# Four attention layers on one core: q and k projected in products of 512 columns, normalized rows in two tiles, maxima woven over the last two steps

## The chip, the cores and the metric

The kernel runs on one core of one Trainium2 chip. The metric is device time in microseconds (us) of one launch; of several runs the median counts. TensorE (PE in the profile) multiplies, and loads the weights of each product first (PEld); VectorE (DVE), ScalarE (ACT) and GpSimd (POOL) work on tiles; SyncE (SP) issues the transfers. Each engine runs its own instructions in the order in which the program wrote them, and waits at an instruction until what it needs is there.

## What is computed

Four layers with a residual connection, alternately of two kinds. A has 32 heads with their own keys and values, B has 32 heads of queries and one head of keys and values. All is float32, with 2048 tokens, a width of 576 and heads of 18.

```python
x = A_x
x = x + _A_ref(_layernorm(x, axis=-1), A_wqkv, A_wo)
x = x + _B_ref(_layernorm(x, axis=-1), B_wq, B_wk, B_wv, B_wo)
x = x + _A_ref(_layernorm(x, axis=-1), A_wqkv, A_wo)
x = x + _B_ref(_layernorm(x, axis=-1), B_wq, B_wk, B_wv, B_wo)
# _A_ref and _B_ref: q, k, v = projections of x
# scores = einsum("bhqd,bhkd->bhqk", q, k) * Dh ** -0.5
# o = einsum("bhqk,bhkd->bhqd", softmax(scores), v);  return o @ wo
```

## The kernel before

**Layout.** The sixteen chunks of 128 tokens lie in `xo`. A layer normalizes them (`norm`, in two stages: `stats` and `scaled`), transposes the result on TensorE (`trans`), projects it to q, k and v, runs the attention of sixteen pairs of heads over four blocks of 512 queries, and multiplies by the output weights (`out_proj`), chunk by chunk, while the chunks of the next layer are already normalized.

**Accuracy.** Each number is split in a rounded part and a rest. A projection therefore has fourteen products (`TERMS`) for each result, with transposed rows of 9 parts of 128 (`split_rows`) against weights of 10 parts. The result leaves PSUM (`project`) as a rounded part by ACT and a rest by VectorE; both go to the DRAM tile `qk_d` (`store`) and come back by head (`load_k`, `load_q`) into the slots of `big`, where the projection's weights lie too. `project(..., filler=True)` uses the PSUM buffers "e" (three) in place of "m" (two), lets ACT copy the result twice and POOL subtract, and so leaves VectorE free.

**The loop before.** It takes 256 tokens at a time (`tt` 0 to 7). Transposed rows have two tiles of 256 tokens, in turn (`xt`). `project(tt, xt, group)` computes one or two results of 128 rows by 256 tokens, next to each other in one PSUM buffer. In A there are nine results (q and k: 1152 rows) a step, and `project_v` adds the values of the step before, four products of 14 terms and 288 columns; in B there are five, and the fifth holds the last queries, the keys and the values, which `v_trans` transposes back. Between the projections stand `trans` of the next step and `norm` of the one after that: in B, `norm(tt + 2, 0)` after the second result group and `norm(tt + 2, 1)` ahead of the third.

**The last steps.** The attention of a layer starts with maxima of scores: `max_pair` multiplies for both heads of a pair (L464, `psm`), and VectorE reduces (L473, `mx`). The first 28 pairs are woven into the projections: `woven(f, left, every)` calls `f` after every so many products (`beat`). In A the fillers (values and the results 1, 2, 3, 5 of the steps 6 and 7) come last; the first eight of them (`FIRST_A`) run by themselves and the others carry the pairs. In B pairs are woven from step 4 (`MAX_B`) on, in an order of blocks (`m_first`) that follows what has been stored. Then come the exponents (L608, `pse`, with ACT's L612) and the products with the values (L633, `oacc`).

**Starts.** Layer 0 loads its weights through `load_a` (part 0, 2, 1; ACT and VectorE split them). In each A layer POOL splits the value weights into `wsm` (`load_wsm`), behind what it has to do for `norm` before, and ahead of what it has to do for `norm` after: it computes `rs`, the root, that `scaled` needs. In the layers 1 to 3 the chunks 0 and 1 are transposed within `out_proj`, at its chunk 14.

Of the kernel before, what the change touches and what calls it, by code (L numbers as in the profile page):

```python
# [18 lines left out]
P = 128  # L19
# [35 lines left out]

FIRST_A = 8
MAX_B = 4
# [15 lines left out]
def tile_kernel(ctx: ExitStack, tc: tile.TileContext, A_x, A_wqkv, A_wo, B_x, B_wq, B_wk, B_wv, B_wo, out):  # L73
# [28 lines left out]
    vbuf = cst.tile([P, NCH * H * (DH + 1)], F32, name="vbuf")  # L102
# [182 lines left out]
    xhs, xts = {}, {}  # L285

    def trans(c):
        tt, u = divmod(c, 2)
        if u == 0:
            xts[tt] = pool.tile([P, 9, 256], F32R, tag="xt", name="xt")  # L290
        xh = xhs.pop(c)
        split_rows(xts[tt][:, :, u * P:(u + 1) * P], *transposed(xh, xh[:, 512:640]))
# [31 lines left out]
    load_x(0)  # L324
    for layer in range(4):
        is_a = layer % 2 == 0
        if is_a:
            v = vbuf.rearrange("p (c h e) -> p c h e", c=NCH, h=H)
        else:
            v = vbuf[:, :NCH * (DH + 1)].rearrange("p (c h e) -> p c h e", c=NCH, h=1)  # L330


        def project(tt, xt, group, filler=False):
            t0 = tt * 256
            ps = (etile if filler else mtile)("psq").rearrange("p (m t) -> p m t", m=2)
            g = len(group)
            n = 114 if not is_a and group[0] == 4 else P
            for k, t in enumerate(group):
                w = wtile(t)
                for j, (xc, wc) in enumerate(TERMS):  # L340
                    nc.tensor.matmul(ps[:n, k, :], w[:, wc, :n], xt[:, xc, :],  # L341
                                     start=j == 0, stop=j == len(TERMS) - 1)
                    beat()
            ev = [ptile("ev", (P, 2, 256), F32R) for _ in range(2)]
            ev_f = [e.bitcast(F32) for e in ev]
            nc.scalar.activation(ev[0][:n, :g], ps[:n, :g], AF.Copy)  # L346
            if filler:
                raw = ptile("evr", (P, 2, 256))
                nc.scalar.activation(raw[:n, :g], ps[:n, :g], AF.Copy)  # L349
                nc.gpsimd.tensor_tensor(ev[1][:n, :g], raw[:n, :g], ev_f[0][:n, :g], op=OP.subtract)  # L350
            else:
                nc.vector.tensor_tensor(ev[1][:n, :g], ps[:n, :g], ev_f[0][:n, :g], op=OP.subtract)  # L352
            if not is_a and group[0] == 4:
                vt = ptile("vt", (P, 256))
                nc.scalar.activation(vt[64:82], ps[64:82, 0], AF.Copy)  # L355
                store(ev_f, 0, 64, 512, 0, t0)
                store(ev_f, 96, 96 + DH, D, 0, t0)
                vts.append((tt, vt))
            else:
                for k, t in enumerate(group):  # L360
                    if t == 4:
                        store(ev_f, 0, 64, 512, k, t0)
                        store(ev_f, 64, P, D, k, t0)
                    else:
                        store(ev_f, 0, P, t * P, k, t0)

        def store(ev_f, r0, r1, c0, k, t0):

            dst = qk_d[c0:c0 + r1 - r0, :, t0:t0 + 256]
            hi, lo = ev_f[0][r0:r1, k, None, :].to_broadcast([r1 - r0, 2, 256]), ev_f[1][r0:r1, k, :]  # L370
# [9 lines left out]
        def v_trans(tt, vt):  # L380
            pv = etile("psv")
            for u in range(2):
                nc.tensor.transpose(pv[:, u * 32:u * 32 + DH], vt[64:82, u * P:(u + 1) * P], ident[64:82, 64:82])
            nc.vector.tensor_copy(v[:, 2 * tt:2 * tt + 2, 0, :DH],
                                  pv[:, :64].rearrange("p (u e) -> p u e", u=2)[:, :, :DH])

        def project_v(tt, xt, u, h, tile_f):
            c = 2 * tt + u
            pv = natural(xt[:, :, u * P:(u + 1) * P], h, tile_f)
            nc.scalar.activation(v[:, c, 16 * h:16 * h + 16, :DH], pv.rearrange("p (e d) -> p e d", d=DH), AF.Copy)  # L390
# [47 lines left out]
        def ops(p):  # L438
# [5 lines left out]
                                   [(0, i, 2) for i in range(4)] + [(0, i, 3) for i in range(4)] +  # L444
                                   [(1, i // 2, i % 2) for i in range(4, 8)] +
# [32 lines left out]
        def max_pair():  # L478
# [4 lines left out]
            if not is_a and m_done[0] == 44:  # L483
                max_store(0, 0)
            elif not is_a and m_done[0] == 52:
                max_rows(0, 0)

        nc.gpsimd.memset(v[:, :, :, DH:], 1.0)
        if layer == 0:
            norm(0, 0)  # L490
            norm(0, 1)
            for part in (0, 2, 1):
                for c in range(5):
                    load_a(c, (part,), nc.scalar, nc.vector)
                if part == 0:
                    load_x(1)
                    trans(0)
                    trans(1)
                elif part == 2:
                    norm(1, 0)  # L500
            load_x(2)
            norm(1, 1)
        else:
            for c in outs:
# [11 lines left out]
        if is_a:  # L516
            groups = [(0, 1), (2, 3), (4, 5), (6, 7), (8,)]
            first, rest = [(6, 7), (8,), (0,), (4,)], [1, 2, 3, 5]
        else:
            groups = [(4,), (0, 1), (2, 3)]  # L520
            first, rest = [], [1, 2, 3]
        fill = []
        for tt in range(8):
            if tt == 0 and is_a:
                for c in range(5):
                    load_wsm(c, A_wqkv[:, 2 * D:])
            elif tt == 0:
                fixed_rows(k_slot(0), True)
                fixed_rows(q_slot(0), False)
            if layer == 0 and tt < 5:  # L530
                load_x(tt + 3)
            gs = groups if tt < 6 else first
            for i, g in enumerate(gs):
                if tt < 6 and i == (3 if is_a else 2):
                    norm(tt + 2, 1)
                if not is_a and tt == MAX_B and i == 2:
                    woven(max_pair, 2, 13)
                elif not is_a and tt > MAX_B and i == 1:
                    woven(max_pair, 4, 13)
                project(tt, xts[tt], g, not is_a and tt >= MAX_B)  # L540
                if is_a and tt == 7 and i == 2:
                    load_k(0, 0, 1792)
                    load_q(0, 0, 512)
                if is_a and 0 < tt < 7 and i < 2:
                    for h in range(2):
                        project_v(tt - 1, xts[tt - 1], i, h, mtile)
# [228 lines left out]
```

## Time and profile before

| what | us |
|---|---|
| runs | 5867.71, 5867.76, 5873.08; median 5867.76 |
| the profiled execution | 5869.39, its span 5867.6 |
| layer 0: to the first exponent | 229.08 |
| a layer's attention (of layer 3) | 1233.07 |
| output projection of layer 0 after its first two chunks, to the projections of layer 1 | 56.57 |
| projections of layer 1 (B) to its first exponent | 107.48 |
| projections of layer 2 (A) to its first exponent | 207.43 |

A row of the timeline gives the start within the span, the length, the engine, the line, the operation, the tiles and their shape, and how many instructions it holds; in square brackets stands how long the engine had been idle before it and what released it. The length reaches to the end of the last one's result, so the time that a run of products takes is read from the start of one row to the start of the next.

### The profile page before, as it was taken

The numbers are of one execution on the slowest core, as the hardware profiler recorded it, in microseconds if no ns is written. First come the engines' busy times: TensorE is split into PE (matmuls) and PEld (weight loads), VectorE is DVE, ScalarE is ACT, GpSimd is POOL, SyncE is SP. The second block draws the span as 40 slices with busy tenths as digits, with TensorE's granted clock in tenths as the row PEclk, the third lists the DMA queues.
The fourth block names the chain that finished last, engine by engine and source line by source line (L and its number), as shares of the span: only waits on it lengthen the run. The fifth ranks groups of instructions, "written<-read, shape, count | busy, mean of one in ns | idle before, by whom it ended". The sixth has DMA issues, their size and how long they took to land. (4 is left out here: it accounts for less than half of the span.)

```text
span 5867.6 us, 136457 instructions
## 1 busy us (share of the span) xinstructions
PE 5806.8 (99%) x55296; PEld 3003.1 (51%) x55296; DVE 5183.2 (88%) x5424; ACT 4622.0 (79%) x8952; POOL 1716.4 (29%) x2209
## 2 busy tenths in 40 slices
PE   8999999999999999999999999999999999999999
PEld 8644444444844444444696444444448444444446
DVE  4799999997599999999647999999976999999995
ACT  2588888888278888888625888888882888888885
POOL 2142232324133232233311323232332323223232
PEclk9999999999999999999999999999999999999999
DMA  6311111111320000000243111111113200000002
GB/s 191 111 43 33 35 31 35 32 31 26 120 65 23 22 20 22 21 21 24 68 137 103 45 35 31 35 32 34 30 33 120 56 23 23 22 23 19 23 14 76
DMA packets 295958, 276.66 MB, mean 47 GB/s; under 512 B 135680, under 2 KB 259896, under 8 KB 285608
## 3 DMA queue, kind: packets, MB, share of 16 engines
q1 hardware_dynamic: 295328, 267.94, 16.6%
q8 instruction: 434, 7.11, 0.5%
q14 instruction: 196, 1.61, 0.1%
HBM read 151.24 MB, written 112.56 MB: 45 GB/s over the span
## 5 line engine op out<-in xcount | busy, mean ns | idle before, releaser
L473 DVE TENSOR_REDUCE mx<-psm 128x2 f32<-128x1024 f32 x4096 | 4768.0, 1217 | 179.2 <-PE psm L464 144.9
L612 ACT ACTIVATE pt<-pse 128x512 f32<-128x512 f32 x8192 | 4314.3, 602 | 543.2 <-PE pse L608 375.4
L608 PE MATMUL pse<-big 64*128 64x512 f32 x8192 | 2447.5, 417 | 3.8 <-DMA big<-m_d 2.3
L633 PE MATMUL oacc<-pt,vbuf 128*19 128x256 f32 (+2 forms) x32736 | 2323.5, 384 | 1.9 <-ACT oc L639 1.9
L464 PE MATMUL psm<-big 62*128 62x512 f32 x8192 | 2297.1, 454 | 6.6 <-DVE mx L473 6.4
L464 PEld LDWEIGHTS psm<-big 62*128 62x128 f32 x8192 | 926.0, 184 | 1461.4 <-DVE mx L473 921.0
L608 PEld LDWEIGHTS pse<-big 64*128 64x128 f32 x8192 | 1187.1, 185 | 286.3 <-ACT pt L612 191.6
L633 PEld LDWEIGHTS oacc<-pt,vbuf 128*19 128x19 f32 x32736 | 676.1, 97 | 1023.1 <-issue 796.4
L139 POOL TENSOR_SCALAR hl<-neg 128x8 fp32r<-128x8 f32 x256 | 50.9, 199 | 2665.6 <-DVE neg L584 2665.6
L656 POOL TENSOR_TENSOR rl<-lt,mone 128x8 f32<-128x8 f32 x256 | 422.9, 1652 | 564.3 <-DMA lt<-os 564.3
L341 PE MATMUL psq<-xt,big 128*128 128x256 f32 (+1 forms) x3136 | 422.1, 290 | 18.6 <-DVE ev L352 11.7
L341 PEld LDWEIGHTS psq<-xt,big 128*128 128x128 f32 (+1 forms) x3136 | 391.4, 192 | 44.0 <-issue 20.7
L346 ACT ACTIVATE ev<-psq 128x512 fp32r<-128x512 f32 (+2 forms) x148 | 73.2, 495 | 370.9 <-PE psq L341 298.9
L139 POOL TENSOR_SCALAR os<-oc 32x512 f32<-32x512 f32 x512 | 313.2, 612 | 130.8 <-ACT oc L639 88.6
L669 POOL TENSOR_TENSOR os<-os,rb 96x512 f32<-96x512 f32 x256 | 328.9, 1285 | 20.3 <-DMA rb<-r_d 19.5
L647 POOL TENSOR_TENSOR os<-os,oc 96x512 f32<-96x512 f32 x256 | 327.3, 1279 | 21.3
L216 PE MATMUL psn<-wsm,ot 128*128 128x288 f32 x1792 | 245.8, 298 | 9.7 <-DVE xo L282 7.3
L216 PEld LDWEIGHTS psn<-wsm,ot 128*128 128x128 f32 x1792 | 241.5, 190 | 17.5 <-issue 11.5
L352 DVE TENSOR_TENSOR ev<-psq,ev 128x512 fp32r<-128x512 f32 (+2 forms) x100 | 59.7, 604 | 168.2 <-ACT ev L346 152.9
L282 DVE TENSOR_TENSOR xo<-psn,xo 128x288 f32<-128x288 f32 x128 | 58.0, 456 | 143.2 <-PE psn L216 142.2
L639 ACT ACTIVATE oc<-oacc 128x512 f32<-128x512 f32 x256 | 157.7, 616 | 28.1 <-PE oacc L633 28.1
L137 ACT ACTIVATE ot<-o 128x512 fp32r<-128x512 f32 (+1 forms) x84 | 42.5, 553 | 135.2 <-PE psn L216 68.1
(54 smaller groups left out, 1127.6 us busy)
## 6 DMA issues: line engine op xcount, KB each, us to landing
big<-qk_d SPq DMA_DIRECT2D x180, 432.0 KB
qk_d<-ev SPq DMA_DIRECT2D x192, 256.0 KB
qk_d<-ev SPq DMA_DIRECT2D x240, 128.0 KB
rb<-r_d SPq DMA_DIRECT2D x512, 36.0 KB
o_d<-os SPq DMA_DIRECT2D x512, 36.0 KB
m_d<-tr SPq DMA_DIRECT2D x1024, 2.0 KB
o<-o_d SPq DMA_DIRECT2D x64, 256.0 KB
big<-m_d SPq DMA_DIRECT2D x512, 4.0 KB
```

The source lines that it names most:

```text
L139: eng.tensor_scalar(dst, src, 1.0, 0.0, op0=OP.mult, op1=OP.add)
L216: nc.tensor.matmul(ps, lhs[:, xc, :], wsm[:, wc, h * 288:(h + 1) * 288], start=i == 0, stop=i == len(TERMS) - 1)
L341: nc.tensor.matmul(ps[:n, k, :], w[:, wc, :n], xt[:, xc, :], start=j == 0, stop=j == len(TERMS) - 1)
L464: nc.tensor.matmul(ps[:, slot], q[b:b + KM, c0:c0 + P], k[b:b + KM, kb * 512:(kb + 1) * 512], start=True, stop=True)
L473: nc.vector.reduce_max(mxs[p, u][:, r0:r1 + 1:r1 - r0], ps, axis=AX.X)
L608: nc.tensor.matmul(e, k[r:r + KE, kc * P:(kc + 1) * P], q[r:r + KE, u * 512:(u + 1) * 512], start=True, stop=True)
L612: nc.scalar.activation(pt, e, AF.Exp, scale=SCALE)
L633: nc.tensor.matmul(oacc[j:j + DH + 1, cs], v[:, kc, 2 * p + a if is_a else 0, :], pts[p, u, i][:, cs], start=kc < 2 and c0 == 0, stop=kc > ...
L639: nc.scalar.activation(oc, oacc, AF.Copy)
L647: nc.gpsimd.tensor_tensor(t[:96], t[:96], oc[:96], op=OP.add)
L656: nc.gpsimd.tensor_tensor(rl, lts.pop((p, u)), mone, op=OP.pow)
L669: nc.gpsimd.tensor_tensor(t[:96], t[:96], rb[:96], op=OP.mult)
```

## The change

A step now takes 512 tokens (`T` 0 to 3), and one product of 512 columns computes what two of 256 did. Transposed rows need two tiles of twice the size. One, `xx`, is a tile of its own and serves the output projection too; the other, `yx`, takes turns with the second half of the values of an A layer (`vy`), so that `vbuf` holds one half only. The values of the chunks 8 to 11 are therefore staged (`vst`) and copied by POOL when `yx` is free. Chunks 0 to 3 are normalized and transposed ahead of the loop. In B the keys and queries are loaded in each step, and pairs of maxima are woven over the steps 2 and 3. In A two fillers run by themselves in place of eight.

```diff
-FIRST_A = 8
-MAX_B = 4
+FIRST_A = 2
...
-    vbuf = cst.tile([P, NCH * H * (DH + 1)], F32, name="vbuf")
+    NV = NCH // 2 * H * (DH + 1)
+    vbuf = cst.tile([P, NV], F32, name="vbuf")
+    xx = cst.tile([P, 2, 9, 256], F32R, name="xx")
...
-        ots_[tt] = ot = pool.tile([P, 9, 256], F32R, tag="xt", name="ot")
+        ots_[tt] = ot = xx[:, tt % 2]
...
+    def xt_of(c):
+        T = c // 4
+        if T not in xts:
+            xts[T] = xx if T % 2 else pool.tile([P, 2, 9, 256], F32R, tag="vy", bufs=1, name="yx")
+        return xts[T][:, c // 2 % 2, :, c % 2 * P:(c % 2 + 1) * P]
...
-        def project(tt, xt, group, filler=False):
-            t0 = tt * 256
-            ps = (etile if filler else mtile)("psq").rearrange("p (m t) -> p m t", m=2)
-            g = len(group)
-            n = 114 if not is_a and group[0] == 4 else P
-            for k, t in enumerate(group):
-                w = wtile(t)
-                for j, (xc, wc) in enumerate(TERMS):
-                    nc.tensor.matmul(ps[:n, k, :], w[:, wc, :n], xt[:, xc, :],
-                                     start=j == 0, stop=j == len(TERMS) - 1)
-                    beat()
+        def project(T, t, filler=False):
+            t0 = T * 512
+            ps = (etile if filler else mtile)("psq")
+            n = 114 if not is_a and t == 4 else P
+            w = wtile(t)
+            for j, (xc, wc) in enumerate(TERMS):
+                nc.tensor.matmul(ps[:n].rearrange("p (u t) -> p u t", u=2), w[:, wc, :n], xts[T][:, :, xc, :],
+                                 start=j == 0, stop=j == len(TERMS) - 1)
+                beat()
...
-            dst = qk_d[c0:c0 + r1 - r0, :, t0:t0 + 256]
+            dst = qk_d[c0:c0 + r1 - r0, :, t0:t0 + 512]
...
         if layer == 0:
-            norm(0, 0)
-            norm(0, 1)
+            for tt in range(2):
+                norm(tt, 0)
+                norm(tt, 1)
+                if tt == 0:
+                    trans(0)
+                    trans(1)
             for part in (0, 2, 1):
                 for c in range(5):
                     load_a(c, (part,), nc.scalar, nc.vector)
                 if part == 0:
-                    load_x(1)
-                    trans(0)
-                    trans(1)
-                elif part == 2:
-                    norm(1, 0)
-            load_x(2)
-            norm(1, 1)
+                    trans(2)
+                    trans(3)
+                load_x({0: 2, 2: 3, 1: 4}[part])
         else:
             for c in outs:
...
-                if c in (9, 11):
-                    norm(0, (c - 9) // 2)
-                if c == NCH - 2:
-                    trans(0)
-                    trans(1)
-                    norm(1, 0)
-            norm(1, 1)
+                if c in (9, 11):
+                    norm((c - 9) // 2, 0)
+                elif c in (10, 12):
+                    norm((c - 10) // 2, 1)
+                if c in (11, 13):
+                    trans(c - 11)
+                    trans(c - 10)
+        norm(2, 0)
+        norm(2, 1)
+        rest = [1, 2, 3, 5] if is_a else [2, 3]
+        for T in range(4):
...
+            if is_a:
+                ts = range(9) if T < 3 else (6, 7, 8, 0, 4)
+            else:
+                ts = (4, 0, 1, 2, 3) if T < 3 else (4, 0, 1)
+            for i, t in enumerate(ts):
+                if not is_a and T == 2 and i == 1:
+                    woven(max_pair, 10, 5)
+                elif not is_a and T == 3:
+                    woven(max_pair, *((2, 7), (4, 3), (4, 3))[i])
+                project(T, t, not is_a and T >= 2)
+                if is_a and T == 3 and i == 2:
+                    load_k(0, 0, 1536)
+                    load_q(0, 0, 512)
+                for tt, j in ((2 * T + 2, 0), (2 * T + 3, 4 if is_a else 2)) if T < 3 else ():
+                    if i in (j, j + 1):
+                        trans(2 * tt + i - j)
+                    if i in (j + 1, j + 2) and tt < 7:
+                        norm(tt + 1, i - j - 1)
+                if not is_a and i < 2:
+                    (load_q if i else load_k)(0, T * 512, T * 512 + 512)
+                if vts and i != 0:
+                    v_trans(*vts.pop())
+            if is_a and T < 3:
+                staged = []
+                for c in range(4 * T, 4 * T + 4):
+                    for h in range(2):
+                        project_v(c, h, mtile, staged if T == 2 else None)
+                if staged:
+                    vs.append(pool.tile([P, NV], F32, tag="vy", bufs=1, name="vy")
+                              .rearrange("p (c h e) -> p c h e", c=NCH // 2, h=H))
+                    nc.gpsimd.memset(vs[1][:, :, :, DH:], 1.0)
+                    for c, h, t in staged:
+                        copy(nc.gpsimd, v_dst(c, h), t.rearrange("p (e d) -> p e d", d=DH))
+        fill = []
+        if is_a:
+            for c in range(12, NCH):
+                for h in range(2):
+                    fill.append((project_v, (c, h, etile)))
+        for t in rest:
+            fill.append((project, (3, t, True)))
+        if is_a:
+            load_k(0, 1536, S)
+            load_q(0, 512, S)
+            for f, args in fill[:FIRST_A]:
+                f(*args)
+            fill = fill[FIRST_A:]
```

`max_store` and `max_rows` of the first block in B come one pair later (after 46 and 54 maxima), `v_trans` turns four chunks at once, and `m_first` lists the pairs in another order.

More of the change, by code (lines that the diff above doesn't have):

```diff
@@ L528, in tile_kernel @@
                 fixed_rows(k_slot(0), True)
                 fixed_rows(q_slot(0), False)
[L530 to L542, printed above, removed]
-                    load_q(0, 0, 512)
-                if is_a and 0 < tt < 7 and i < 2:
-                    for h in range(2):
-                        project_v(tt - 1, xts[tt - 1], i, h, mtile)
-                if tt < 7 and i in ((1, 2) if is_a else (0, 1)):
-                    trans(2 * tt + 2 + i - is_a)
-                if tt < 6 and i == 1:
-                    norm(tt + 2, 0)
+            if is_a:
+                ts = range(9) if T < 3 else (6, 7, 8, 0, 4)
+            else:
+                ts = (4, 0, 1, 2, 3) if T < 3 else (4, 0, 1)
```

131 lines of the change are left out of this document (50 added, 81 removed).

## The prediction

> **What bounds the kernel now.** I read the page's busy shares first, then the busy time of each engine in stretches, then TensorE's timeline where the diff works. In the rows of stretches below the columns are: length, then busy time (and instructions) of PE, PEld, DVE, ACT and POOL, then granted clock, DMA share, GB/s.
>
> ```profile
> PE 5806.8 (99%) x55296; PEld 3003.1 (51%) x55296; DVE 5183.2 (88%) x5424; ACT 4622.0 (79%) x8952; POOL 1716.4 (29%) x2209
> ```
> ```profile
> 0.00:229.08 229.08, 212.82 (x1594) 200.13 (x1594) 105.33 (x196) 58.62 (x134) 37.76 (x83) 0.99 0.54 172
> 77.80:101.30 23.50, 23.50 (x194) 23.50 (x193) 8.50 (x19) 5.85 (x14) 1.57 (x4) 1.00 0.56 177
> 196.51:229.08 32.57, 31.89 (x172) 20.53 (x170) 31.35 (x30) 4.95 (x14) 3.78 (x8) 1.00 0.34 109
> 1477.60:1534.17 56.57, 53.67 (x406) 53.15 (x403) 29.60 (x65) 10.99 (x23) 9.86 (x15) 1.00 0.23 69
> 1534.17:1641.65 107.48, 100.04 (x705) 85.20 (x704) 77.01 (x143) 31.07 (x78) 24.37 (x42) 0.97 0.47 150
> 2943.89:3151.32 207.43, 205.04 (x1585) 193.51 (x1584) 91.32 (x161) 48.64 (x114) 28.92 (x57) 1.00 0.45 146
> 4563.53:5796.60 1233.07, 1231.80 (x12200) 547.62 (x12200) 1176.02 (x1129) 1099.85 (x2111) 377.47 (x463) 1.00 0.10 24
> ```
> The last row is an attention phase: some 1235 us in each of four layers, which the change doesn't enter. It works in the projections (229 us in layer 0, 107 in a B layer, 207 in layer 2) and in the output projection ahead of them (57). There too TensorE is the bound: one 256-token step of an A layer (second row) keeps it busy for all of its 23.5 us. So a saved product counts in full, and so does each new wait of TensorE.
>
> **The change, part by part.** *(1) The products.* 3136 products of 256 columns become 1568 of 512.
>
> ```profile
> 43.12 3.87 PE L216 MATMUL psn<-wsm,xt 128*128 128x288 f32 x28
> 46.83 3.48 PE L341 MATMUL psq<-xt,big 128*128 128x256 f32 x28
> 50.15 3.87 PE L216 MATMUL psn<-wsm,xt 128*128 128x288 f32 x28
> 53.85 0.60 PE L208 MATMUL ps<-ident,xh 128*128 128x128 f32 x4
> ...
> 54.32 3.57 PE L341 MATMUL psq<-xt,big 128*128 128x256 f32 x28
> ```
> ```profile
> 1652.59 0.62 PE L608 MATMUL pse<-big 64*128 64x512 f32 x2
> ...
> 1654.71 0.40 PE L608 MATMUL pse<-big 64*128 64x512 f32 x1
> ```
> From start to start, 28 products of 256 columns take 3.32 us (46.83 to 50.15), 118.6 ns each; of 288 columns, 3.71 and 3.70 us, 132.3 each. The line through both has 0.428 ns a column and 9 ns fixed, so 228 at 512. No product of 512 columns over all 128 rows is in the trace. The nearest are those of the exponents, on 64 rows: two span 0.62 us where one lasts 0.40, so they start some 0.23 apart. I take 229. The bounds are 219 (the fixed part vanishes) and 237.2 (two of the old ones; the columns now lie in two pieces of 256). Gain: 1568 x (237.2 - 229) = 12.9 us; by the bounds 28.5 and nothing.
>
> The Trainium skill (TensorE: Matmul & The Clock Gate, "Wait — 56ns, not 53.3ns?") puts warm products N/2.4 + 2.5 ns apart, 215.8 at 512, by which this term would be 33.6 us. The trace disagrees at 256 (118.6 against 109.2) and at 288. The same page ("Back-to-back issue gap") gives 131 ns for 512 columns with their weight loads, which would save 167 us; the 0.23 us above speaks against it.
>
> *(2) Maxima in the A layers.* 28 pairs of maxima were woven after every fourth product of the last eight fillers; now after every fifth of the last ten, two going ahead instead of eight.
>
> ```profile
> 1623.99 0.85 PE L341 MATMUL psq<-xt,big 128*128 128x256 f32 x5
> 1624.77 0.50 PE L464 MATMUL psm<-big 62*128 62x512 f32 x2
> 1625.20 0.85 PE L341 MATMUL psq<-xt,big 128*128 128x256 f32 x5
> ```
> Five products and a pair take 1.21 us, so a pair adds 1.21 - 5 x 0.119 = 0.62. The old stretch should take 28 x 0.62 + 56 x 0.132 + 56 x 0.119 = 31.4; it took 32.57 with VectorE busy for 31.35, which set its end. With five longer products a pair TensorE sets it again: 1.1 us in each A layer, -2.2.
>
> *(3) Their operands.* In the A layers only two fillers, no longer eight (14.1 us by the durations above), go between the loads of q and k and the first maximum.
>
> ```profile
> 182.55 0.78 SPq L403 DMA_DIRECT2D big<-zeros  x1
> ...
> 189.08 1.07 SPq L412 DMA_DIRECT2D big<-qk_d  x2
> ```
> Issuing the fixed rows and both loads takes SP 7.6 us, here behind stores that need some 2 us after the last product that reads these slots; with 2 us to land (estimate, no row prints it) the rows stand 11.6 us after it. TensorE arrives after two projections (6.4), two value products (3.7) and five more (0.7), at 10.8. A wait of 0.8 each (bounds 0 and 3): +1.6. The eight value tiles staged for the copy by POOL hide: POOL has nothing else there, and its eight copies (0.43 each, as in the first row under (5)) end long before the values are read.
>
> *(4) Output projection.* Chunks 0 to 3 are transposed inside it, formerly 0 and 1.
>
> ```profile
> 1528.24 0.60 PE L208 MATMUL ps<-ident,xh 128*128 128x128 f32 x4
> ...
> 1530.26 0.33 PE L209 MATMUL ps<-ident,xh 128*128 128x128 f32 x1 [0.87 <-DVE xt L202]
> 1530.34 3.96 PE L216 MATMUL psn<-wsm,ot 128*128 128x288 f32 x28
> ```
> Two chunks in a row cost 2.1 us, for the second waits for VectorE to free a PSUM buffer; a chunk by itself, among projections, costs 0.47 (53.85 to 54.32) and 0.08 on the next product. I add 0.4 because VectorE has both normalizations there: 2.5 - 1.1 = 1.4 in three layers, +4.2.
>
> *(5) Starts of the A layers.* Scaling rows needs POOL's rs. POOL splits the ten value weights first.
>
> ```profile
> 2944.30 0.43 POOL L139 TENSOR_SCALAR wsm<-raw 128x288 fp32r<-128x288 f32 x1
> ...
> 2958.36 0.22 POOL L249 TENSOR_SCALAR rs<-mv 128x1 f32<-128x1 f32 x1
> ```
> ```profile
> 2961.90 3.59 PE L341 MATMUL psq<-xt,big 128*128 128x256 f32 x28 [1.70 <-DVE ev L352]
> ```
> The splits take 14.0 us, VectorE stood behind rs, and so did the evacuation (ev) that TensorE needed. Now two more chunks are normalized ahead of the splits, which start some 3.5 us after the output projection (estimate: a last addition and the statistics of two chunks) instead of 0.4. They end at 17.5; with rs and 0.59 us of scaling chunk 6 is ready at 18.9, and ev, behind chunk 7, at 20.8, while TensorE is done with five projections and two transpositions at 17.2, and a third takes 0.55: a wait of 3.0 in place of 2.0. In layer 0:
>
> ```profile
> 10.88 9.04 PE L341 MATMUL psq<-xt,big 128*128 128x256 f32 x56
> ...
> 37.03 6.26 PE L341 MATMUL psq<-xt,big 128*128 128x256 f32 x28 [5.67 <-DVE ev L352]
> ...
> 77.83 2.38 PE L341 MATMUL psq<-xt,big 128*128 128x256 f32 x18
> ```
> ```profile
> 16.84 2.38 DVE L161 TENSOR_TENSOR big<-raw,big 128x384 fp32r<-128x384 f32 x5
> ```
> A chunk takes VectorE some 2.7 us (8.50 in a step, less 4.5 evacuations of 0.69, halved); two more ahead of the first product, with handovers, move it from 10.9 to 18.9. Then come two more splits (4.8), statistics, rs at 27, POOL's 14 us, scaling and ev: the sixth projection starts at 44.4, and four of those (13.6) and eight value products (14.8) end at 72.9. The old kernel had done the same work at 77.83 + 0.55 - 56 x 0.1186 = 71.7. Without the 1.0 that (1) counts, +2.2; bounds -2 and +6. With the clock, below, (5) is +6.2.
>
> *(6) The B layers.* In the new order of instructions norm's second half stands directly ahead of the transposition that reads it, in steps 0 to 2, behind ev of the third projection.
>
> ```profile
> 50.39 0.60 ACT L346 ACTIVATE ev<-psq 128x512 fp32r<-128x512 f32 x1 [2.96 <-PE psq L341]
> ...
> 51.02 0.69 DVE L352 TENSOR_TENSOR ev<-psq,ev 128x512 fp32r<-128x512 f32 x1 [6.33 <-ACT ev L346]
> ```
> ```profile
> L256 DVE TENSOR_SCALAR xh<-xo,mv,rs 128x576 f32<-128x576 f32 x64 | 37.9, 593 | 12.4 <-POOL rs L250 12.2
> ```
> From the last product: 0.24 to ACT, 0.60, 0.69 on VectorE, 0.59 to scale. TensorE, with the transposition at its head and the next projection behind it, waits 2.1 us in steps 0 and 1. In step 2 evacuation is ACT's and POOL's, but VectorE has maxima. There the waits for the three "e" buffers of PSUM stay, as these show:
>
> ```profile
> 1578.66 3.59 PE L341 MATMUL psq<-xt,big 128*128 128x256 f32 x28 [0.60 <-ACT vt L355]
> ...
> 1583.43 0.29 PE L383 MATMUL psv<-ident,vt 18*128 18x18 f32 x2 [0.63 <-ACT evr L349]
> 1584.65 2.18 PE L341 MATMUL psq<-xt,big 128*128 128x256 f32 x13 [0.92 <-DVE xt L202]
> ```
> I count 1.4, 0.95, 0.75, 1.4 and 0.95: where ACT's three copies (0.60 each) or two stand against a 0.47 us transposition, and where a maximum and the scaling do. With 1.1 in step 3, 0.6 for switches and four value transpositions at 0.75, the new waits are 4.2 + 5.4 + 4.7 = 14.3. The old ones: 107.48 less 560 x 0.1186, 28 x 0.62 and 14 x 0.55 leaves 16.0, clock included. For waits touch the clock:
>
> ```profile
> 1582.46:1585.87 3.41, 1.86 (x16) 1.00 0.74 240
> 1585.87:1589.28 3.41, 3.41 (x15) 0.50 0.44 152
> ...
> 1599.52:1602.94 3.42, 2.26 (x16) 1.00 0.48 164
> ```
> (PE alone.) A slice of 3.41 us with 1.86 busy is followed by one at a clock of 0.50, which loses 1.7; one with 2.26 is not. A wait of 2.1 brings this on where it falls in one slice: I take 6 in 10, 1.2 slices a layer, and 1.3 in step 2: 4.3. Together 18.6 against 16.0: +2.6, twice, +5.2. For (5) I take 1.6 in layer 0 and 1.4 in layer 2, a slice each but for a small chance: 2.2 + 1.0 + 1.6 + 1.4 = 6.2.
>
> Stores are half as many, twice as large, and SP waits for nothing more in sum; the loads of q and k in the B layers reach the third product of step 3 some 2 us early.
>
> **Sum.** -12.9 - 2.2 + 1.6 + 4.2 + 6.2 + 5.2 = +2.1. The profiled run took 5869.4 (span 5867.6 and 1.8 around it), 1.6 above the median of 5867.8; so 5871.5 profiled, 5870 as a median.
>
> **The rivals.** *The fixed part vanishes*: behind a long stream the weight load is hidden and products start 219 ns apart. For it: both pairs of rows that give the 9 ns are of short streams. Against: 0.23 us between the exponents' products. 15.7 us less, 5854. 14 in 100. Together with waits that never halve the clock (2 x 4.3 + 3.0 = 11.6 less) it is 5842: 6 in 100. By the page's 215.8 it would be 5849, and by its 131 some 5716, which no row bears out.
>
> *No gain in the products*: a column costs what it did, or reading two pieces costs a second start; 237.2 each, +12.9, 5883. It decides from 235. For it: the row that I lean on has half the rows. 12 in 100.
>
> *The waits take over* (slower): in step 2 of the B layers VectorE serves maxima, statistics, scaling and transposed rows together, and each of its waits pulls the next slice to a clock of 0.50. Six more such slices, three a layer, are 10.2 us: 5880; with the output projection's pairs (1528 to 1531 us has little left) 5885. It decides from the sixth. Against: waits of 0.6 to 0.9 in separate slices left the clock alone. 22 in 100.
>
> **How the numbers follow.** The forecast, within 0.2% (11.7 us, about what a measurement of this kernel tells from no change), has 46 in 100: 5856 to 5879. Faster by more: 14 + 6 = 20. Slower by more: 12 + 22 = 34. The range takes in all but 2 in 10: 5852 to 5890.
>
> **What would show it.** Products of 512 start 229 ns apart within 2, or (1) is wrong. In each B layer TensorE waits some 2 us for xh ahead of a transposition twice, and the granted clock is 0.50 in two or three slices. The first projection starts near 19 us, and one near 44 follows a wait for ev. A layer 2 gains, the B layers lose. The prediction is wrong if the time leaves 5856 to 5879, most likely by the start distance of the long products or by slices at half clock.

## The result and the profile after

The changed kernel takes 5896.66 us (median of six runs, 5891.29 to 5911.20), the kernel before on the same chip 5867.74: 1.0052 times as long, 95% interval 1.0039 to 1.0065. That is 29 us slower, and 7 above the upper end of the forecast range. The profiled execution is the longest of the six (5911.20, span 5909.4), so what follows explains 41.8 us of span, more than the median shows.

Busy time by stretches of the changed kernel, with the columns of the prediction: layer 0 to the first exponent; the output projection of layer 0 behind its first two chunks; the projections of layer 1 (B); of layer 2 (A); the attention of layer 3.

```profile
0.00:241.59 241.59, 221.11 (x1088) 179.84 (x1090) 105.85 (x189) 54.60 (x119) 38.86 (x87) 0.93 0.47 161
1490.78:1554.61 63.83, 57.96 (x417) 57.28 (x414) 32.60 (x73) 12.40 (x27) 10.15 (x15) 0.95 0.21 61
1554.61:1656.00 101.39, 92.76 (x416) 61.94 (x414) 74.63 (x129) 26.65 (x56) 21.59 (x35) 1.00 0.46 155
2965.51:3186.85 221.34, 214.63 (x1071) 174.52 (x1070) 87.44 (x146) 43.84 (x95) 30.80 (x60) 0.92 0.38 135
4601.40:5837.65 1236.25, 1234.81 (x12200) 548.89 (x12200) 1175.58 (x1129) 1100.21 (x2111) 378.63 (x463) 1.00 0.10 24
```
Against the same stretches before: layer 0 is 12.5 us longer, layer 2 13.9, the output projection 7.3, the attention 3.2; the B layer is 6.1 shorter. The other 11 us lie in the same kinds of stretches of the other layers. The two A layers stand out by their granted clock (a share of full speed; in these traces it is 1.00 or 0.50 at any one time), on average 0.93 and 0.92 where it was 0.99 and 1.00.

The place is the first maximum. SyncE's timeline, then TensorE's, in layer 0:

```profile
176.24 0.79 SPq L418 DMA_DIRECT2D big<-zeros  x1
177.09 2.08 SPq L421 DMA_DIRECT2D big<-ones  x2
179.27 0.69 SPq L418 DMA_DIRECT2D big<-zeros  x1
180.02 1.15 SPq L421 DMA_DIRECT2D big<-ones  x2
181.21 0.86 SPq L427 DMA_DIRECT2D big<-qk_d  x2
182.17 1.42 SPq L418 DMA_DIRECT2D big<-zeros  x2
183.63 0.96 SPq L427 DMA_DIRECT2D big<-qk_d  x2
```
```profile
183.79 1.35 PE L218 MATMUL psn<-wsm,xx 128*128 128x288 f32 x9
189.38 1.10 PE L479 MATMUL psm<-big 62*128 62x512 f32 x2 [4.24 <-DMA big<-qk_d]
190.41 1.57 PE L218 MATMUL psn<-wsm,xx 128*128 128x288 f32 x5
```
The last load is issued at 184.59 and the first maximum starts at 189.38; TensorE has stood for 4.24 us. In layer 2 the wait is 3.90 us (L479 at 3131.60). What came after each wait is in the stretches:

```profile
185.20:188.80 3.60, 0.00 (x0) 0.00 (x0) 0.00 (x0) 0.00 (x0) 0.00 (x0) 1.00 0.98 272
188.80:216.10 27.30, 26.72 (x84) 18.34 (x84) 14.64 (x12) 1.66 (x4) 0.00 (x0) 0.50 0.23 75
216.10:241.59 25.49, 25.49 (x109) 15.36 (x109) 18.75 (x18) 4.32 (x9) 4.26 (x5) 1.00 0.24 93
...
3131.10:3165.20 34.10, 33.60 (x105) 22.87 (x105) 18.39 (x15) 2.07 (x5) 0.00 (x0) 0.50 0.17 55
```
For 27.3 us in layer 0, and 34.1 in layer 2, the clock stays at 0.50 although TensorE is busy for 98% of the time. In the kernel before, a stretch at 0.50 was one slice of 3.41 us (two at the start of layer 0). During the wait itself the DMA share is 0.98: the 16 DMA engines are busy all through it, so the bytes bear on its end, and not the latency alone.

### The profile page after: what moved, and what is told of

Its sections match the earlier page's. It is cut to its first block, busy times and chain, and to the rows that moved or that the text cites. A ratio compares the mean times of both kernels' runs of the same rounds, so it can differ in the third digit from the quotient of the medians.

```text
span 5909.4 us, 132735 instructions
## 1 busy us (share of the span) xinstructions
PE 5827.2 (99%) x53728; PEld 2930.1 (50%) x53728; DVE 5184.6 (88%) x5400; ACT 4611.6 (78%) x8888; POOL 1719.9 (29%) x2207
## 4 chain that ended last, share of the span: by engine, by line
PE 95%; POOL 1%; DVE 1%; DMA 1%; issue 1%; ACT 1%; SPq 1%; POOLq 0%; ACTq 0%; DVEq 0%
PE oacc L645 36%; PE psm L479 31%; PE pse L620 16%; PE psq L352 6%; PE psn L218 6%; DVE mx L488 0%; PE ps L210 0%; POOL wsm L163 0%; DMA raw<-in_B_wk_dram 0%; DMA o<-o_d 0%; DMA raw<-in_A_wqkv_dram 0%; ACT pt L624 0%; POOL wsm L141 0%; SPq L152 0%; POOL big L163 0%
## 5 line engine op out<-in xcount | busy, mean ns | idle before, releaser
L479 PE MATMUL psm<-big 62*128 62x512 f32 x8192 | 2307.0, 456 | 12.5 <-DMA big<-qk_d 4.2
L645 PE MATMUL oacc<-pt,vbuf 128*19 128x384 f32 (+1 forms) x24560 | 1756.7, 384 | 1.9 <-ACT oc L651 1.9
L479 PEld LDWEIGHTS psm<-big 62*128 62x128 f32 x8192 | 930.0, 184 | 1488.8 <-DVE mx L488 928.7
L645 PEld LDWEIGHTS oacc<-pt,vbuf 128*19 128x19 f32 x24560 | 500.9, 97 | 774.1 <-issue 596.2
L645 PE MATMUL oacc<-pt,vy 128*19 128x256 f32 x8176 | 592.8, 384 | 0.0
L357 ACT ACTIVATE ev<-psq 128x512 fp32r<-128x512 f32 (+1 forms) x112 | 67.0, 598 | 361.3 <-PE psq L352 268.5
L218 PE MATMUL psn<-wsm,xx 128*128 128x288 f32 x2240 | 337.6, 312 | 11.3 <-DVE xo L284 11.3
L218 PEld LDWEIGHTS psn<-wsm,xx 128*128 128x128 f32 x2240 | 322.4, 201 | 32.2 <-issue 27.2
L645 PEld LDWEIGHTS oacc<-pt,vy 128*19 128x19 f32 x8176 | 177.2, 98 | 250.7 <-issue 202.1
L363 DVE TENSOR_TENSOR ev<-psq,ev 128x512 fp32r<-128x512 f32 (+1 forms) x84 | 57.9, 691 | 215.9 <-ACT ev L357 202.7
L352 PE MATMUL psq<-yx,big 128*128 128x512 f32 (+1 forms) x784 | 202.6, 409 | 6.9 <-ACT vt L366 2.6
L352 PE MATMUL psq<-xx,big 128*128 128x512 f32 (+1 forms) x784 | 202.2, 402 | 0.0
```

The source lines that it names most:

```text
L218: nc.tensor.matmul(ps, lhs[:, xc, :], wsm[:, wc, h * 288:(h + 1) * 288], start=i == 0, stop=i == len(TERMS) - 1)
L352: nc.tensor.matmul(ps[:n].rearrange("p (u t) -> p u t", u=2), w[:, wc, :n], xts[T][:, :, xc, :], start=j == 0, stop=j == len(TERMS) - 1)
L357: nc.scalar.activation(ev[0][:n], ps[:n], AF.Copy)
L479: nc.tensor.matmul(ps[:, slot], q[b:b + KM, c0:c0 + P], k[b:b + KM, kb * 512:(kb + 1) * 512], start=True, stop=True)
L645: nc.tensor.matmul(oacc[j:j + DH + 1, cs], v_of(kc)[:, 2 * p + a if is_a else 0, :], pts[p, u, i][:, cs], start=kc < 2 and c0 == 0, stop=k ...
```

## The experiments

The theory: the short cover leaves a wait at the first maximum, the wait puts the clock to 0.50, and the value products with a pair of maxima between every five let it stay there. The rivals: that weave lowers the clock by itself; or the loss lies elsewhere (output projection, starts, B layers). All runs in one table. "Wait" is that of the first maximum in layer 0, "at 0.50" the stretch behind it in layers 0 and 2 of the profiled execution; the ratio is against the kernel before on the same chip.

| kernel | median us | lowest, highest | ratio, 95% interval | wait | at 0.50 |
|---|---|---|---|---|---|
| changed | 5896.66 | 5891, 5911 | 1.0052, 1.0039 to 1.0065 | 4.24 | 27.3, 34.1 |
| constant rows early | 5867.34 | 5865, 5873 | 1.0006, 0.9997 to 1.0015 | none | none |
| cover of four | 5872.97 | 5869, 5878 | 1.0015, 1.0005 to 1.0024 | 0.86 | none |
| wide products first | 5884.32 | 5878, 5890 | 1.0033, 1.0021 to 1.0046 | 3.27 | 6.8, 6.8 |
| old kernel, cover of two | 5885.80 | 5883, 5889 | 1.0035, 1.0022 to 1.0048 | 8.14 | 13.7, 10.2 |
| no cover | 5892.62 | 5891, 5899 | 1.0046, 1.0033 to 1.0059 | 8.06 | 10.2, 13.7 |
| ones last | 5882.52 | 5873, 5895 | 1.0026, 1.0016 to 1.0036 | 1.88 | 10.2, 6.8 |
| + transpositions ahead | 5873.23 | 5869, 5886 | 1.0014, 1.0006 to 1.0023 | 2.1 | 17.1, 3.4 |
| + second scaling ahead | 5871.32 | 5862, 5881 | 1.0008, 1.0000 to 1.0017 | 1.6 | 23.9, 3.4 |
| ones last, cover of four | 5871.10 | 5868, 5875 | 1.0009, 1.0000 to 1.0018 | none | none |
| + transpositions ahead | 5865.69 | 5861, 5870 | 0.9998, 0.9989 to 1.0007 | none | none |
| + second scaling ahead | 5861.84 | 5856, 5866 | 0.9993, 0.9984 to 1.0002 | none | none |
| the same, cover of three | 5860.41 | 5856, 5881 | 0.9992, 0.9983 to 1.0001 | none | none |

**Constant rows early.** The zeros and ones of the first pair of heads are issued ahead of the last 512 tokens' projections. There they land on weights still in use (the slots hold the projections 6 to 8), so that these tokens' rows are not the reference's; the work is the same.

```diff
-            if t0 == 0 and is_a and p < 3:
+            if t0 == 0 and is_a and 0 < p < 3:
...
-            elif T == 0:
+            if T == (3 if is_a else 0):
                 fixed_rows(k_slot(0), True)
                 fixed_rows(q_slot(0), False)
```


> The changed kernel, with the eight transfers of constant rows of the first pair of heads (zeros and ones) of an A layer issued ahead of the last 512 tokens' first projection instead of between its stores and the loads of q and k. Weave and cover are as in the changed kernel. Theory (the wait of 4.2 us at the first maximum puts the clock to half, and the maxima woven at every fifth value product keep it there for 27 and 34 us): loads issued about 5 us earlier, the wait at the first maximum under 1 us in both A layers, no stretch at 0.50 behind it, and the time falls by about 34 us (8 of waits, 25 of clock) to 5858 to 5868. Rival (the weave at every fifth product with narrow value products sets the clock to half by itself): the waits go but the stretches at 0.50 stay, 5885 to 5890. Rival (the loss lies in the output projections, the starts and the B layers): 5888 to 5897, whatever the clock does behind the first maximum.

It took 5867.34 us. TensorE's timeline at the first maximum, and the stretches of layer 0, of its woven part, and of layer 2:

```profile
185.07 0.50 PE L479 MATMUL psm<-big 62*128 62x512 f32 x2
185.51 0.93 PE L218 MATMUL psn<-wsm,xx 128*128 128x288 f32 x5
186.37 0.50 PE L479 MATMUL psm<-big 62*128 62x512 f32 x2
```
```profile
0.00:225.86 225.86, 208.36 (x1089) 170.90 (x1090) 105.84 (x189) 54.65 (x119) 38.75 (x87) 0.99 0.51 172
184.50:225.86 41.36, 41.36 (x197) 26.36 (x197) 33.39 (x29) 6.37 (x14) 4.26 (x5) 1.00 0.28 101
...
2946.22:3149.07 202.85, 200.11 (x1070) 164.97 (x1070) 87.47 (x146) 43.78 (x95) 30.68 (x60) 1.00 0.41 147
```
No wait, full clock over the same weave, and 15.7 and 18.5 us less in the two layers, 34.2 of the 41.8. The rival of the weave falls, and most of the loss doesn't lie elsewhere.

**Cover of four.** `FIRST_A = 4` in the changed kernel, pairs at every fourth product.

> The changed kernel with four instead of two value products ahead of the first maximum; the others carry a pair of maxima at every fourth instead of every fifth product. Theory: 2 x 14 products of 0.132 us more of cover, 3.7 us, leave a wait of about 0.5 us in each A layer; no stretch at 0.50; 5860 to 5870. Rival (the weave itself sets the clock): maxima lie closer, the share of value products is smaller, so the stretches at 0.50 stay or grow, 5885 to 5905. Rival (loss elsewhere): 5888 to 5897.

A wait of 0.86 us in layer 0 and no stretch at 0.50. The median, 5872.97, is 3 above what was expected and 5.6 above that with the constant rows early. In the two profiled executions the layers 0 and 2 are 1.0 us longer each than there (226.88 and 203.82); the pairs at every fourth product are one difference, the wait is another, and the rest was not followed up.

**Wide products first.** The cover and the wait stay, but of the woven products the four projections of 512 columns lead.

```diff
             fill = fill[FIRST_A:]
+            fill = fill[-4:] + fill[:-4]
```


> The changed kernel with the same two value products ahead of the first maximum, so the same wait of about 4.2 us, but of the woven products the four projections of 512 columns come first and the six value products behind them. Theory (the wait sets the clock to half, and only the narrow value products between the maxima keep it there): the wait stays, the clock is at 0.50 for one to three slices of 3.4 us behind it and full from then on, 5870 to 5880. Rival (after such a wait the clock stays at half whatever is woven): both stretches stay at 27 to 34 us, 5890 to 5900. Rival (the weave of value products sets the clock by itself): a stretch at 0.50 comes behind the projections, when the value products carry the maxima, 5885 to 5900.

Layer 0 in stretches, behind a wait of 3.27 us:

```profile
188.90:195.70 6.80, 6.80 (x16) 3.89 (x16) 2.46 (x2) 0.54 (x2) 0.00 (x0) 0.50 0.58 202
195.70:232.62 36.92, 36.89 (x179) 23.54 (x179) 30.90 (x28) 6.28 (x14) 5.56 (x6) 1.00 0.38 124
```
Two slices, and full clock from then on, also where the value products carry maxima. The wait starts the half clock, and what is woven behind it bears on how long it lasts. At 5884.32 it is 12 us faster than the changed kernel; 5870 to 5880 had been expected.

**The old kernel with a cover of two**, `FIRST_A = 2` there, pairs at every seventh product.

> The kernel before with two instead of eight value products ahead of the first maximum; a pair of maxima at every seventh product. Theory: the first maximum waits for the loads of q and k in both A layers, 4 us or more, and the clock stays at half behind it for as long as narrow value products are woven: 5885 to 5905. Rival (the wait costs itself and one slice of 3.4 us at half clock): 5876 to 5884. Rival (there is no such wait in the old order of transfers, the cover was never needed): 5862 to 5870.

```profile
194.45 1.24 PE L464 MATMUL psm<-big 62*128 62x512 f32 x2 [8.14 <-DMA qk_d<-ev]
```
```profile
188.60:202.20 13.60, 7.75 (x25) 5.72 (x26) 3.51 (x3) 0.42 (x1) 0.00 (x0) 0.50 0.53 144
```
(The releaser is the transfer that the trace saw last in that queue.) The wait is twice as long as in the changed kernel, and the stretch at 0.50, nearly half of it inside the wait, is half as long. It had been expected to last as long as value products are woven; it ended before that in both layers, here at 202.06, while value products go on until 203.04 and come again, at full clock, from 214.67. The kernel is 21 us slower than before (5865.20 on that chip) from this line alone: the cover of eight had carried the old kernel past its loads.

**No cover.** `FIRST_A = 0` in the changed kernel, pairs at every sixth product.

> The changed kernel with no value product ahead of the first maximum; a pair of maxima at every sixth product. Theory (the wait starts the half clock, the weave decides how long it lasts): the wait grows by 3.7 us to about 8, the stretches at 0.50 last between those at every fifth product (27 and 34 us) and those at every seventh in the old kernel (14 and 10 us), so 15 to 27 us: 5890 to 5905. Rival (the length grows with the wait): over 35 us each, 5910 to 5925.

```profile
186.60:196.80 10.20, 7.29 (x23) 5.42 (x24) 3.68 (x3) 0.41 (x1) 0.00 (x0) 0.50 0.75 220
```
With a wait of 8.06 us the stretches are 10.2 and 13.7 us, shorter than expected, and the rival (the length grows with the wait, over 35 us each) falls; the weave is another here too, so the wait was not varied alone. A wait of 8 us is no dearer here than one of 4 us (ratios 1.0046 and 1.0052).

**Ones last.** The maxima read rows 0 to 61 of a slot; the ones lie behind them and are now issued after the loads (`one_rows`, the four transfers of ones taken out of `fixed_rows`).

```diff
         def load_k(p, t0=0, t1=S):
             if t0 == 0 and is_a and p < 3:
-                fixed_rows(k_slot(p), True)
+                fixed_rows(k_slot(p), p > 0)
...
             load_q(0, 512, S)
+            one_rows(k_slot(0))
```


> The changed kernel with only the order of the constant rows changed: the four transfers of ones of the first pair of heads, which the maxima do not read, are issued behind the loads of q and k instead of ahead of them. By the SyncE rows of the changed kernel (2.08 and 1.15 us for the two pairs of ones) the loads are issued 3.3 us earlier. Theory: the wait at the first maximum falls from 4.2 to about 1 us, no stretch at 0.50 of over 7 us behind it, 5864 to 5871. Rival (any wait at that place locks the clock): the stretches of 27 and 34 us stay, 5885 to 5895.

```profile
186.94 0.96 PE L483 MATMUL psm<-big 62*128 62x512 f32 x2 [1.88 <-DMA qk_d<-ev]
187.83 1.57 PE L218 MATMUL psn<-wsm,xx 128*128 128x288 f32 x5
189.33 0.79 PE L483 MATMUL psm<-big 62*128 62x512 f32 x2
190.06 1.57 PE L218 MATMUL psn<-wsm,xx 128*128 128x288 f32 x5
```
The wait is 1.88, not 1, and that is enough for 10.2 us at 0.50; the median of 5882.52 lies between what the theory and what the rival expected. Here a pair with five products takes 2.23 us (187.83 to 190.06); at full clock, in the first experiment, 1.30 (185.07 to 186.37): 0.93 lost a pair. The eleven runs spread over 22 us, at mean clocks from 0.997 down to 0.992, the slowest runs at the lowest.

**Transpositions ahead, second scaling ahead**, each on top of the one before.

```diff
+                if c in (11, 13):
+                    trans(c - 11)
+                    trans(c - 10)
                 if c in (9, 11):
                     norm((c - 9) // 2, 0)
                 elif c in (10, 12):
                     norm((c - 10) // 2, 1)
-                if c in (11, 13):
-                    trans(c - 11)
-                    trans(c - 10)
```


> As the kernel with the ones last, and in the output projection of layers 0 to 2 the transpositions of a pair of chunks are issued ahead of the next pair's statistics, not behind them. Theory (the second transposition waits 2.2 us because the split of the first stands behind 2 us of statistics on VectorE, and a slice at half clock follows): the wait falls under 1 us, the time from the last values' product to the next first projection falls from 63 to 64 us to 58 to 60 in each of the three, 9 to 15 us together: 5852 to 5861. Rival (the next pair's scaled rows come later by the same amount and the last transposition waits instead): within 3 us of the kernel with the ones last.

```diff
+                if not is_a and T < 3 and i == 2:
+                    norm(2 * T + 3, 1)
                 project(T, t, not is_a and T >= 2)
...
-                    if i in (j + 1, j + 2) and tt < 7:
+                    if i in (j + 1, j + 2) and tt < 7 and (is_a or j or i < 2):
```


> As the kernel with the transpositions ahead, and in the B layers the second pair's scaling is issued ahead of the third projection of a step, not behind it. Theory: the waits of 2.16 us ahead of the transposition in steps 0 and 1 go (2 x 2 x 2.16 = 8.6 us over both B layers), and the one of about 1 us in step 2; the first projection to the first exponent falls from 101.4 to 96 to 98 us in each; 5 to 9 us less than the kernel with the transpositions ahead: 5844 to 5855. Rival (VectorE holds the projection's eviction back and TensorE waits for a free buffer instead): 0 to 4 us slower than that kernel.

Both came out 12 to 27 us above what was expected, in part because the ones last had not ended the stretch at 0.50 (17.1 and 23.9 us in layer 0). With that in them, differences of a few us can't be read; so the three were run again with a cover of four.

> The kernel with the ones last, and four instead of two value products ahead of the first maximum (3.7 us more of cover, a pair of maxima at every fourth product). With the ones last alone the first maximum still waited 1.9 us for data in both layers, and its runs spread from 5873 to 5895 us as the mean clock went from 0.997 to 0.992. Theory (it is the wait, down to one of 2 us, that starts the half clock, and the value products woven with maxima that let it last): no wait, no stretch at 0.50 behind the first maximum, the spread shrinks to under 10 us, 5863 to 5871. Rival (the more frequent maxima or the change of order bring half clock by themselves): a stretch of 7 us or more behind the first maximum, runs up to 5890.

> As the kernel with the ones last and four products of cover, and the transpositions of the output projection ahead of the next statistics. With the A layers' stretch at half clock out of the way the step shows by itself: 1.1 us less of waiting and one slice of half clock (1.7 us) less in each of three layers, and more where a second slice followed: 4 to 9 us less than the kernel with the ones last and four products of cover. Rival (a half-clock slice comes elsewhere in its place): within 2 us of it.

> As the kernel with four products of cover and the transpositions ahead, and the second pair's scaling of a B layer ahead of the third projection. In the run without that cover the first projection to the first exponent took 100.1 instead of 102.9 us in both B layers, so 3 to 5.6 us less than the kernel with four products of cover and the transpositions ahead; with the steps together 5854 to 5862, which is faster than the kernel before by 0.1 to 0.2 per cent. Rival (the gain without the cover was the spread of the half clock): within 2 us of that kernel, and the same as the kernel before.

5871.10, 5865.69, 5861.84. The first, at the upper edge of what was expected, shows no wait and no stretch in both A layers, and its eleven runs lie within 6.5 us instead of 22. This is its woven part of layer 0:

```profile
184.00:225.80 41.80, 41.80 (x200) 26.47 (x199) 32.45 (x29) 6.52 (x14) 4.26 (x5) 1.00 0.36 119
```
The transpositions are worth 5.4, the scaling 3.9, both in the ranges of these second runs; the times of 5852 to 5861 and 5844 to 5855, expected at first, were not reached. TensorE in the output projection of the second, and in the first step of a B layer of the third:

```profile
1515.32 0.60 PE L210 MATMUL ps<-ident,xh 128*128 128x128 f32 x4
1516.79 0.33 PE L211 MATMUL ps<-ident,xh 128*128 128x128 f32 x1 [0.87 <-DVE yx L204]
```
```profile
1541.67 3.53 PE L352 MATMUL psq<-yx,big 128*128 128x512 f32 x14
1546.01 0.63 PE L210 MATMUL ps<-ident,xh 128*128 128x128 f32 x4 [0.81 <-DVE xh L258]
```
The second transposition waits 0.87 us (2.23 in the changed kernel), the one behind the scaling 0.81 (1.99). A B layer went to 100.1 us, not to the 96 to 98 that had been expected.

**Cover of three**, all else as in the last.

> As the kernel with the ones last, the transpositions ahead and the second scaling ahead, with three instead of four value products ahead of the first maximum, so that a pair of maxima comes at every fifth product again. Without that third product the first maximum waited 1.9 us; 14 products of 0.132 us are 1.85, so the cover is just met. Theory (it takes a wait to start the half clock, and the weave at every fifth product is the cheaper one): no stretch at 0.50 behind the first maximum in most runs, 5857 to 5862, 0 to 5 us less than with four. Rival (the cover is too narrow, and runs in which the data come a little later fall to half clock): a spread of over 12 us, up to 5880, median 5863 to 5870.

5860.41, with ten runs within 5856 to 5865 and one of 5881 at a mean clock of 0.993: the cover is just met, and not always. (In layer 2 of the profiled execution the first maximum waits 0.77 us, without a stretch at 0.50.) The median is the theory's, the spread the rival's. The expectation was wrong in one point: nine fillers have 126 products for 28 pairs, so the pairs still came at every fourth. These last two kernels have the lowest medians, and both intervals still touch 1: that they are faster than before, by 0.07 and 0.08%, is not shown.

## Why the prediction was wrong

**Step (3) failed: the operands of the first maximum.** The prediction put the wait at 0.8 us a layer (bounds 0 and 3) and counted nothing for the clock. The wait was 4.24 and 3.90. Of the 3.4 us between, 0.75 is issue (8.35 from 176.24 to 184.59 against 7.6); the rest is the landing, 4.8 us from 184.59 to 189.38 where 2 was assumed. That estimate left out the size: the first loads bring 2 x 54 rows of 1536 and of 512 columns of 4 bytes, 885 KB, and at the 272 GB/s of the row 185.20:188.80 that alone takes 3.3 (an estimate, for stores move in that row too). The larger part is the clock. At 0.93 a pair and 2.23 us a pair, 27.3 us lose 11.4 and 34.1 lose 14.2; with both waits that is 33.7, and the first experiment got back 34.2.

The prediction's view of the clock was one slice per wait, as in the stretches it quoted. The Trainium skill (TensorE: Matmul & The Clock Gate, "What's actually happening") has the same: half clock after an idle window of about 3.4 us, full clock after a busy one. The two values and the length of a slice agree with the traces here (1.00 and 0.50, 3.41 us); the release doesn't (26.72 of 27.30 us busy, at 0.50), nor does the start (1.58 us of waiting were enough in the run with the second scaling ahead).

**(1) was right.** Products of 512 columns, in TensorE's timeline of layer 0:

```profile
72.62 3.37 PE L352 MATMUL psq<-xx,big 128*128 128x512 f32 x14
75.82 0.60 PE L210 MATMUL ps<-ident,xh 128*128 128x128 f32 x4
...
76.28 3.46 PE L352 MATMUL psq<-xx,big 128*128 128x512 f32 x14
79.58 0.60 PE L210 MATMUL ps<-ident,xh 128*128 128x128 f32 x4
```
228.6 ns each in the first run; the second begins behind a transposition, and with that start in it gives 235.7. Over the whole trace, at full clock and within a run, the median distance is 231, where that of 256 columns was 119 before: 1568 x (2 x 119 - 231) is a gain of 11 us for the 12.9 forecast. 229, within 2, was forecast; both rivals about the products (219, and 237.2, which decided from 235) fall. **(2) was right**: at full clock a pair takes 1.30 - 5 x 0.132 = 0.64 (forecast 0.62), and in the stretch 184.50:225.86 TensorE is busy throughout, VectorE for 33.39 of 41.36.

**(4) was mis-sized**: 2.5 us more for each output projection, less 1.1 in the layer behind it. The three took 7.3, 3.7 and 5.1 more. TensorE in the first, then VectorE:

```profile
1533.06 0.60 PE L210 MATMUL ps<-ident,xh 128*128 128x128 f32 x4
1535.90 0.33 PE L211 MATMUL ps<-ident,xh 128*128 128x128 f32 x1 [2.23 <-DVE yx L204]
```
```profile
1533.31 0.81 DVE L247 BATCH_NORM_STATS2 st<-xo 128x6 f32<-128x288 f32 x2
...
1535.20 0.64 DVE L204 TENSOR_TENSOR yx<-ps,yx 128x512 fp32r<-128x512 f32 x1
```
"VectorE has both normalizations there" had been priced at 0.4. In fact the next pair's statistics are issued ahead of the split of the first chunk, and the split that frees the PSUM buffer starts 1.9 us later. Of the 7.3, the added pair takes 3.5 (1532.52 to 1535.98), a wait in the middle of the projection is 0.7 longer (2.76 at 1508.64, before 2.03 at 1494.75), and two slices at 0.50 follow these waits (1509.8 and 1537.1; before none), 1.6 each; no slice had been counted in (4). The swap of the two was worth 5.4 us in all three.

**(5) was right in its steps, and a little high.** TensorE at the start of layer 0:

```profile
17.54 5.33 PE L352 MATMUL psq<-yx,big 128*128 128x512 f32 x14
...
44.09 3.52 PE L352 MATMUL psq<-yx,big 128*128 128x512 f32 x14 [0.44 <-DVE ev L363]
```
The forecast was 18.9 for the first and 44.4, behind ev, for the sixth. With the wait at the first maximum away, layer 0 reaches its first exponent 3.2 us earlier than before and layer 2 gains 4.6, where (1), (2) and (5) made 1.4 and 2.8, and the 1.1 of (4) lies in layer 2 besides.

**(6): the waits were right, the slices at 0.50 were fewer.**

```profile
1562.72 3.53 PE L352 MATMUL psq<-yx,big 128*128 128x512 f32 x14
1568.24 0.63 PE L210 MATMUL ps<-ident,xh 128*128 128x128 f32 x4 [1.99 <-DVE xh L258]
...
1583.84 3.47 PE L352 MATMUL psq<-xx,big 128*128 128x512 f32 x14
1589.36 0.63 PE L210 MATMUL ps<-ident,xh 128*128 128x128 f32 x4 [2.04 <-DVE xh L258]
```
Waits of 1.99 and 2.04 us ahead of a transposition (forecast 2.1), yet no slice at 0.50 in layer 1 (clock 1.00 in its row) and one in layer 3 (4513.48), where 2.5 were counted in each, for 4.3 us. The prediction's condition, that such a wait must fall in one slice, agrees with this. The changes of the clock in this trace lie whole numbers of 3.4133 us apart (1267 of them from 188.80 to 4513.48); an edge of these slices cuts both waits of layer 1 in two (1567.78 and 1588.26), while a wait of 1.99 us in layer 3 lies whole in the slice from 4510.07 to 4513.48, and the next one is at 0.50. That 6 in 10 were counted, and 1.3 more in step 2, was too many. So layer 1 took 6.1 us less and layer 3 4.5, where 0.8 less was forecast (2.6 more by this step, less 2.3 of (1) and the 1.1 of (4)). Part of it was given back: two slices at 0.50 came at the start of the attention behind (1659.9 to 1666.8), two at that of layer 3 (from 4605.6), where none had stood, and the attention of layer 3 took 3.2 more.

**The sum and the rivals.** Without the wait of step (3) the change stands at 5867.34 against 5865.20, 2.1 slower, where the sum less the 1.6 of (3) gives 0.5. That is partly luck, since (4) was too low (16.1 more in the three output projections, where 7.5 was forecast) and (5) and (6) were too high. The rival "the waits take over" had the sign and the mechanism, a wait of TensorE that pulls the clock to 0.50, but looked for six slices in the B layers; eight and ten came in the A layers, from two waits.

## What to carry to other kernels

Work that is put between the issue of a load and its first use has to cover issue, bytes over the DMA rate and latency together; when it is shortened, count all three from the trace. A wait of TensorE can cost several times itself (here 4.24 us, and 11.4 more at half clock) when short products and maxima over half the rows follow it; with the long ones over all rows behind the wait, the kernel was 12 us faster. If runs of one kernel spread by far more than usual, look at the mean clock of each run before differences of a few us are read.

## What was not expected of the hardware

The granted clock stayed at 0.50 for 27.3 and 34.1 us of work in which TensorE was busy for 98%, and the same instructions ran at 1.00 when no wait stood ahead of them. Waits of 1.88 and 1.58 us ahead of the maxima were enough to start it, for 10.2 and 23.9 us. Among products of 512 columns in the B layers a wait of 1.99 us that lay whole in a slice brought one slice at 0.50, and waits of 1.99 and 2.04 that an edge of the slices cut in two brought none; nor did one of 2.04 of which 1.94 lay in one slice (transpositions ahead with a cover of four, at 1568.78). The length varied from one execution to another: with a pair at every fifth product 3.4 to 34.1 us, at every sixth and seventh 10.2 to 13.7 (some of it inside the wait), with 512 columns first 6.8 twice. The maxima use 62 of the 128 rows, and the longest stretches were seen where the fewest full products lie between them; that this share decides was not tried by itself, and what sets the length stays open.
